# Loads of Q, K and V on a second DMA queue, ordered by a plan of both queues, in a fused attention and MLP kernel

The kernel runs on one core of one Trainium2 chip. The metric is device time of one execution in microseconds (us), median of several runs; lower is better. An execution of the kernel before takes about 333 us.

## The reference

Sliding-window attention, then an MLP whose activation is s * relu(h)^2 + b:

```python
# q, k, v: (batch 8, heads 8, seq 576, head_dim 64), float32
scores = (q @ k.T) / 8, masked to |i - j| <= 32
attn   = softmax(scores) @ v                # (8, 8, 576, 64)
x      = attn, heads side by side           # 4608 tokens x 512
h      = x @ w_in                           # 4608 x 2048
out    = (s * relu(h)**2 + b) @ w_out       # 4608 x 512
```

## The kernel before

All work is recorded as tasks (engine, cost, what it reads and writes, a key for urgency) and a planner in Python turns them into one fixed order for each engine. The order of each list is fixed when the program is built; on the chip each engine works through its list and waits on semaphores.

The dense part works in blocks of up to 512 tokens: `w<-xt,win` (TensorE, first product), `r<-w` (ScalarE, relu), `gt<-r` (VectorE, square), `o<-wout,gt` (TensorE, second product), `outs<-o` (VectorE), store. Attention is planned about two blocks ahead and stands between the dense matmuls. A batch has five units of 128 queries. From batch 2 on a batch goes this way:

```python
def load_v(b, t, key, waits=()):                 # five a batch
    add("sp", dma VST[0:n, t] <- v[b, :, 128*t : 128*t+n], 650.0, key=key, dma=("l", n // 2, 21.0), waits=waits)

def chunk(b, t0, n, key, names="qk"):            # (t0, n) = (0, 512) and (512, 64), for q and k each
    ...
    add("sp", dma stg <- src[b, :, t0:t0+n], 500.0, key=key - 20.0,
        waits=[paced(b, PACE[...])], dma=("l", np_ // 2, 53.0))
    add("dve", tensor_copy nat <- stg, 110 + 0.53 * 2048, key=key, slack=3000.0)       # f32 to bf16
    add("sp", dma transpose QT or KTR <- nat, 2200.0 if n > 64 else 1200.0, key=key + 0.1, dma=("t", np_, 22.0))
    if name == "k":
        add("pool", tensor_copy KT <- KTR, ...)  # GpSimd puts K into order, 128 columns at a time
```

`paced(b, u)` makes a load wait for an attention unit of an earlier batch, since its buffers are in use until then. After the scores come exp (ScalarE), mask (VectorE), the product with V (TensorE, `avn`), and the normalisation into one of NXN = 3 XN buffers (VectorE). From batch 3 on a DMA transpose brings XN into XT, where the dense part reads it.

The planner takes, again and again, the open task that can start first (ties by key). It guesses when a load lands with one FIFO for all hardware DMAs:

```python
def plan(self, rounds=5):
    for _ in range(rounds):
        self._order()     # start = max(engine free, ready); ready of a load's user: self.land + 100 + slack
        self._rings()     # land = start + cost + 300, then served one after the other, + 1100
```

The softmax here doesn't subtract the row's maximum and nothing guards it: scores larger than these inputs give would overflow.

## Time and profile before

| | before |
|---|---|
| median of all runs beside the changed kernel's, us | 333.0 (332.0 to 334.6) |
| span of the profiled run, us | 332.1 |
| TensorE busy, us | 305.5 |
| TensorE idle, 0 to 60 / 60 to 160 / 160 to 320 us | 13.2 / 9.4 / 0.5 |
| TensorE at half clock between 100 and 200 us | 2 x 3.4 us |
| VectorE busy / ScalarE busy / GpSimd busy, us | 204.7 / 141.1 / 59.0 |

The prediction below shows the lines of the profile that carry this. Read the idle time by stage, not as a share of the whole: the change doesn't touch the loads of batches 0 and 1 and the weights, and after 160 us TensorE hardly waits.

### The profile page before, as it was taken

To read this page: it belongs to the slowest core of one execution; us is meant where nothing else is said; L and a number is where in the kernel's file an instruction comes from. 1 tells how busy PE (TensorE), PEld (TensorE's weight loads), DVE (VectorE), ACT (ScalarE), POOL (GpSimd) and SP (SyncE) were. 2 spreads that over 40 slices of the span, in tenths; PEclk is the share of its full clock that TensorE was granted. 3 is DMA by queue.
4 is the path that set the end of the run, shared out by engine and by line. 5 is a ranking of instruction groups with operands and counts; after the bars stand their busy time and mean duration, and the time that the engine had idled before them with its cause. 6 is when DMAs were issued, how large, how long until landed. Compare 5 with 4: busy or idle time off the path is not lost.

```text
span 332.1 us, 8135 instructions
## 1 busy us (share of the span) xinstructions
PE 305.5 (92%) x3452; PEld 162.2 (49%) x3452; DVE 204.7 (62%) x396; ACT 141.1 (42%) x219; POOL 59.0 (18%) x72
## 2 busy tenths in 40 slices
PE   3687999899989996988999999999999999999995
PEld 3565787654445443433445444444544444444442
DVE  2865768857887884858667865995654443333321
ACT  4644574246435653543444444444544323333300
POOL 3446444005050004100500600040000000000000
PEclk9999999999999999899799999999999999999999
DMA  7999999899999966998899879973121111100021
GB/s 255 288 307 353 335 273 343 145 200 238 197 179 310 222 139 116 287 149 172 245 211 172 208 210 201 169 192 113 45 59 49 49 43 44 53 33 34 34 84 74
DMA packets 104581, 56.71 MB, mean 171 GB/s; under 512 B 77216, under 2 KB 96160, under 8 KB 104544
## 3 DMA queue, kind: packets, MB, share of 16 engines
q1 hardware_dynamic: 104544, 56.18, 72.8%
q8 instruction: 27, 0.44, 0.6%
q14 instruction: 10, 0.08, 0.1%
HBM read 36.70 MB, written 9.44 MB: 139 GB/s over the span
## 4 chain that ended last, share of the span: by engine, by line
PE 58%; DMA 28%; DVE 6%; issue 3%; SPq 2%; POOL 1%; ACT 1%; DVEq 0%
PE o L815 28%; PE w L797 24%; DMA stg<-in_k_dram 7%; DMA vst<-in_v_dram 6%; DMA stg<-in_moe_w_out_dram 5%; DMA xt<-xn 3%; PE avn L597 3%; DMA stg<-in_moe_w_in_dram 2%; DMA qt<-nat 2%; DVE gt L806 2%; DVE nat L504 2%; DMA ktr<-nat 1%; PE o L838 1%; PE sc L541 1%; DVE xn L619 1%
## 5 line engine op out<-in xcount | busy, mean ns | idle before, releaser
L815 PE MATMUL o<-wout,gt 128*128 128x512 bf16 (+1 forms) x640 | 146.2, 361 | 2.8 <-DVE gt L806 1.8
L797 PE MATMUL w<-xt,win 128*128 128x512 bf16 (+3 forms) x704 | 147.9, 346 | 0.9 <-ACT xt L631 0.9
L804 ACT ACTIVATE r<-w 128x512 bf16<-128x512 f32 (+2 forms) x152 | 87.2, 574 | 111.0 <-PE w L797 90.9
L806 DVE TENSOR_TENSOR gt<-r 128x512 bf16<-128x512 bf16 (+2 forms) x152 | 68.9, 459 | 69.8 <-ACT r L804 69.3
L815 PEld LDWEIGHTS o<-wout,gt 128*128 128x128 bf16 x640 | 61.6, 98 | 65.9 <-DVE gt L806 2.3
L797 PEld LDWEIGHTS w<-xt,win 128*128 128x128 bf16 x704 | 60.8, 100 | 58.5 <-issue 2.4
L518 POOL COPY kt<-ktr 128x512 bf16<-128x512 bf16 (+1 forms) x30 | 31.8, 1059 | 135.2 <-DMA ktr<-nat 134.1
L567 ACT ACTIVATE ex<-sc 128x1024 bf16<-128x1024 f32 (+1 forms) x35 | 35.7, 1021 | 35.3 <-PE avn L597 33.9
L828 DVE SCALAR_TENSOR_TENSOR outs<-o,sb,cvec 128x512 f32<-128x512 f32 (+1 forms) x40 | 27.4, 690 | 13.0 <-PE o L815 13.0
L504 DVE CAST nat<-stg 128x2048 bf16<-128x2048 f32 (+1 forms) x24 | 29.7, 1246 | 7.2 <-DMA stg<-in_k_dram 6.0
L597 PE MATMUL avn<-vb,ex 64*64 64x65 bf16 x976 | 22.1, 199 | 8.4 <-DVE xn L619 4.5
L571 DVE TENSOR_TENSOR ex<-ex,mask 128x1024 bf16<-128x1024 bf16 (+1 forms) x35 | 25.8, 739 | 2.4 <-ACT ex L567 1.1
L619 DVE TENSOR_TENSOR xn<-avn,rec 128x512 bf16<-128x512 f32 (+1 forms) x34 | 23.3, 686 | 4.7 <-DMA xt<-xn 3.9
L597 PEld LDWEIGHTS avn<-vb,ex 64*64 64x64 bf16 x976 | 14.4, 108 | 23.5 <-issue 8.7
L445 DVE CAST vb<-vst 128x512 bf16<-128x512 f32 (+1 forms) x32 | 14.5, 456 | 8.3 <-DMA vst<-in_v_dram 8.3
L541 PE MATMUL sc<-qt,kt 64*64 64x128 bf16 x504 | 14.9, 217 | 0.0
L617 DVE RECIPROCAL rec<-avn 128x8 f32<-128x8 f32 (+1 forms) x34 | 6.8, 200 | 8.1 <-PE avn L597 8.1
L465 PE MATMUL w<-ident,nat 64*64 64x64 bf16 x144 | 5.4, 239 | 6.2 <-ACT nat L458 4.5
L541 PEld LDWEIGHTS sc<-qt,kt 64*64 64x64 bf16 x504 | 9.8, 107 | 1.3 <-issue 0.9
L426 POOL CAST win<-stg 128x1024 bf16<-128x1024 f32 x8 | 8.5, 1068 | 8.9 <-DMA stg<-in_moe_w_in_dram 8.8
L631 ACT COPY xt<-avn 128x512 bf16<-128x512 bf16 (+1 forms) x9 | 4.8, 537 | 11.6 <-PE avn L626 11.6
L465 PEld LDWEIGHTS w<-ident,nat 64*64 64x64 bf16 x144 | 4.6, 151 | 6.9 <-ACT nat L458 4.5
(62 smaller groups left out, 96.8 us busy)
## 6 DMA issues: line engine op xcount, KB each, us to landing
vst<-in_v_dram SPq DMA_DIRECT2D x32, 256.0 KB, 5.4
out_dram<-outs SPq DMA_DIRECT2D x32, 256.0 KB, 2.2
stg<-in_q_dram SPq DMA_DIRECT2D x6, 1024.0 KB, 6.6
stg<-in_k_dram SPq DMA_DIRECT2D x6, 1024.0 KB, 11.2
stg<-in_moe_w_in_dram SPq DMA_DIRECT2D x8, 512.0 KB, 7.6
stg<-in_moe_w_out_dram SPq DMA_DIRECT2D x8, 512.0 KB, 9.1
stg<-in_q_dram SPq DMA_DIRECT2D x8, 288.0 KB, 5.7
stg<-in_k_dram SPq DMA_DIRECT2D x8, 288.0 KB, 6.1
```

Of the source, the lines that this page charges most:

```text
L504: add("dve", lambda e, stg=stg, nat=nat: e.tensor_copy(nat.rearrange("p (i h d) -> p h i d", h=H, i=4), stg.rearrange("p (h i d) -> p h i ...
L518: add("pool", lambda e, c=c, w=w: e.tensor_copy(KT[slot][:, :, c:c + w].rearrange("p a (s i) -> p a s i", i=4), KTR[slot][:, :, :, c // 4: ...
L541: fns = [lambda e, pr=pr, j=j, hp=hp: e.matmul(SC[64 * (j % 2):64 * (j % 2) + 64, hp, pr * 128:pr * 128 + 128], lhsT=KT[slot][64 * hp:64 * ...
L567: add("act", lambda e, dst=flat_dst, src=flat_src: e.activation(dst, src, AF.Exp, bias=0.0, scale=0.125), 190 + 0.833 * 512 * len(hs), rea ...
L571: add("dve", lambda e, flat=flat, mask=mask: e.tensor_tensor(flat, flat, mask, ALU.mult), 130 + 0.53 * 512 * len(hs), reads=[("E", ei, hp, ...
L597: return [lambda e: e.matmul(av[64 * x:64 * x + 64, h, 0:D + 1], lhsT=buf[64 * g:64 * g + 64, h % 2, h // 2, c:c + 64], rhs=VB[slot][64 * ...
L619: add("dve", lambda e: e.tensor_tensor(XN[xi][0:p1, :].rearrange("p (a c) -> p a c", a=H), av[0:p1, :, 0:D], REC[ri][0:p1, :].rearrange("p ...
L797: add("pe", [lambda e, g=g, kc=kc: e.matmul(wt[:, g, :], lhsT=WIN_BF[:, kc, (f0 + g) * 128:(f0 + g + 1) * 128], rhs=XT[:, kc, t0 % XR:t0 % ...
L804: add("act", lambda e: e.activation(rt, wt, AF.Relu, bias=0.0, scale=1.0), 190 + 0.833 * ng * nt, reads=[("W", wb)], writes=[("R1", rb)], ...
L806: add("dve", lambda e: e.tensor_tensor(GT[gs][:, f0:f0 + ng, g0:g0 + nt], rt, rt, ALU.mult), 130 + 0.53 * ng * nt, reads=[("R1", rb)], wri ...
L815: add("pe", [lambda e, fc=fc: e.matmul(O[:, ob, 0:cn], lhsT=GT[gs][:, fc, g0:g0 + 128], rhs=WOUT_BF[:, fc, c0:c0 + cn], start=(fc == 0), s ...
L828: add("dve", lambda e: e.scalar_tensor_tensor(OUTS[us][:, 0:cn], O[:, ob, 0:cn], SB128[:, 0:1], CVEC[:, c0:c0 + cn], ALU.mult, ALU.add), 2 ...
```

## The change

Its intent: the later loads shall not stand in one queue with transposes and stores, and the planner shall know what two queues do. Core of the diff (the planner's new inner functions and a few constants are cut; NTILE and the like are unchanged):

```diff
-LAG = 2
+LAG = 1                      # units between scores and their product with V
-PACE = ((-1,-1,-1,-1),(-2,-2,-2,-2),(-2,-2,-2,-2))
+PACE = ((-1, -1, -1),) * 3
+LATE = 2                     # batches from here on load from ScalarE
+CASTE = (("pool", "pool"), ("dve", "dve"))
+SLACK = (1000.0, 2000.0, 3000.0, 3000.0)
+    RING, CALM, ISSUE, WRITE = 112.0, 40.0, 1400.0, 600.0
-    def plan(self, rounds=5): ... _rings ... _order ...
+    def plan(self):
+        rings, clock, room = {"sp": [], "act": []}, [0.0], {}
+        ...  # serve(): both rings' heads share the DMA engines; a load's user becomes ready when it is served
+                    if s == "act" and t.dma is not None:
+                        at = max(at, space(s, self.CALM))     # a load only into a nearly drained ring
+        ...
+            full = max(st, space(t.stream, self.RING))        # an issue holds its engine while the ring is full
-        NSTG, NNAT, NEX, NXN, NR1, NOUT, XR = 8, 6, 5, 3, 3, 6, 2048
+        NSTG, NNAT, NEX, NXN, NR1, NOUT, XR = 8, 6, 5, 5, 3, 5, 2048
+        def late(b):
+            return "sp" if b < LATE else "act"
         def load_v(b, t, key, waits=()):
-            add("sp",
+            add(late(b),
-        def chunk(b, t0, n, key, names="qk"):
+        def piece(b, parts, key, waits):        # q 512 | k 512 | q 64 and k 64 in one staging tile
+            add(late(b), [dma of each part], ...)
+            for x in (0, 1):                    # the cast in two halves of 1024 columns
+                eng = CASTE[min(b, 3) - 2][x]
+                add(eng, tensor_copy nat half x <- stg, ...)
+            ...                                 # transposes stay on "sp"
```

More of the change, by code (lines that the diff above doesn't have):

```diff
@@ L30 @@
 XPE = 3
-PACE = ((-1,-1,-1,-1),(-2,-2,-2,-2),(-2,-2,-2,-2))
+PACE = ((-1, -1, -1),) * 3
+CASTS = 20.0
+LATE = 2
+AFTERV = 4
+KTV = 0
+CASTE = (("pool", "pool"), ("dve", "dve"))
+SLACK = (1000.0, 2000.0, 3000.0, 3000.0)
 PACEV = ((-1,-1,0,0,1),(0,0,1,1,2),(0,0,1,1,2))
@@ L97, in add @@
         return t
-    def plan(self, rounds=5):
-        self.land = {}
-        for _ in range(rounds):
-            self._order()
-            self._rings()
-    def _rings(self):
-        jobs = {"hw": [], "sw": []}
-        for t in self.order:
-            if t.dma is not None:
-                r = "sw" if t.stream == "pool" else "hw"
-                jobs[r].append([t, t.start + t.cost + (300.0 if r == "hw" else 700.0), float(t.dma[1])])
-        now, at = 0.0, {"hw": 0, "sw": 0}
-        while any(at[r] < len(jobs[r]) for r in jobs):
-            head = {r: jobs[r][at[r]] for r in jobs if at[r] < len(jobs[r])}
-            live = {r: j for r, j in head.items() if j[1] <= now}
-            if not live:
-                now = min(j[1] for j in head.values())
-                continue
-            cost = sum(j[0].dma[2] for j in live.values())
-            step = min(j[2] for j in live.values()) * cost
-            for r, j in head.items():
-                if r not in live:
-                    step = min(step, j[1] - now)
-            now += step
-            for r, j in live.items():
-                j[2] -= step / cost
-                if j[2] <= 1e-6:
-                    self.land[j[0].n] = now + 1100.0 - j[0].start
-                    at[r] += 1
-    def _order(self):
+    def plan(self):
         free = {s: 600.0 for s in self.STREAMS}
@@ L140, in _order @@
         order = []
-        while len(order) < len(self.tasks):
-            best = None
-            for s in self.STREAMS:
-                for t in open_[s]:
-                    c = (max(free[s], t.ready), t.key, t.n)
-                    if best is None or c < best[0]:
-                        best = (c, t)
-            assert best is not None, "a cycle"
-            (st, _, _), t = best
-            open_[t.stream].remove(t)
-            t.start = st
-            free[t.stream] = st + t.cost
-            t.fin = st + t.cost
-            if t.dma is not None:
-                t.fin = st + self.land.get(t.n, t.cost + 1800.0 + t.dma[1] * t.dma[2])
-            order.append(t)
-            for u in t.next:
-                u.left -= 1
-                if u.left == 0:
-                    open_[u.stream].append(u)
+        rings, clock, room = {"sp": [], "act": []}, [0.0], {}
@@ new lines, in serve @@
+        def serve(rings, now, until, jobs=None):
+            while now < until - 1e-6:
+                live = {r: q[0] for r, q in rings.items() if q and q[0][1] <= now + 1e-6}
+                later = [q[0][1] for q in rings.values() if q and q[0][1] > now + 1e-6]
+                if not live:
+                    if not later:
+                        return None, until
+                    now = min(later + [until])
+                    continue
+                cost = sum(j[0].dma[2] for j in live.values())
+                step = min([j[2] * cost for j in live.values()] + [x - now for x in later] + [until - now])
+                now += step
+                for r, j in live.items():
+                    j[2] -= step / cost
+                    if j[2] < 1e-4:
+                        rings[r].pop(0)
+                        return j[0], now
+            return None, until
@@ new lines, in space @@
+        def space(s, most):
+            if (s, most) not in room:
+                copy, now = {r: [list(j) for j in q] for r, q in rings.items()}, clock[0]
+                while sum(j[2] for j in copy[s]) > most + 1e-3:
+                    head = copy[s][0]
+                    over = sum(j[2] for j in copy[s]) - most
+                    if over >= head[2]:
+                        _, now = serve(copy, now, 1e9)
+                    else:
+                        want = head[2] - over
+                        while copy[s] and copy[s][0] is head and head[2] > want + 1e-6:
+                            _, now = serve(copy, now, now + 50.0)
+                room[s, most] = now
+            return room[s, most]
@@ L161, in _order, with release @@
+        def release(t):
             for u in t.users:
@@ L173, in _order @@
                     open_[u.stream].append(u)
+        while len(order) < len(self.tasks):
+            best = None
+            for s in self.STREAMS:
+                for t in open_[s]:
+                    at = max(free[s], t.ready)
+                    if s == "act" and t.dma is not None:
+                        at = max(at, space(s, self.CALM))
+                    c = (at, t.key, t.n)
+                    if best is None or c < best[0]:
+                        best = (c, t)
+            st = best[0][0] if best else 1e9
+            done, clock[0] = serve(rings, clock[0], max(st, clock[0]))
+            room.clear()
+            if done is not None:
+                done.fin = clock[0] + self.WRITE
+                release(done)
+                continue
+            assert best is not None, "a cycle"
+            t = best[1]
+            open_[t.stream].remove(t)
+            t.start = st
+            free[t.stream] = t.fin = st + t.cost
+            order.append(t)
+            for u in t.next:
+                u.left -= 1
+                if u.left == 0:
+                    open_[u.stream].append(u)
+            if t.dma is None:
+                release(t)
+                continue
+            full = max(st, space(t.stream, self.RING))
+            if t.dma[0] == "t":
+                free[t.stream] = full + t.cost
+            else:
+                free[t.stream] = max(st + t.cost, full)
+            rings[t.stream].append([t, (full if t.dma[0] == "t" else st) + self.ISSUE, float(t.dma[1])])
+            room.clear()
         self.order = order
+        while any(rings.values()):
+            done, clock[0] = serve(rings, clock[0], 1e9)
+            done.fin = clock[0] + self.WRITE
     def emit(self, sems):
@@ L432, in paced @@
             return land["av", b - 1, u] if u >= 0 else land["av", b - 2, NUNIT + u]
+        def late(b):
+            return "sp" if b < LATE else "act"
         def load_v(b, t, key, waits=()):
             n = min(128, S - 128 * t)
-            add("sp",
+            add(late(b),
                 lambda e: e.dma_start(VST[0:n, t, :, :], v[b, :, 128 * t:128 * t + n, :].rearrange("h p d -> p h d")),
-                650.0, writes=[("VST", t)], key=key, dma=("l", n // 2, 21.0), waits=waits)
+                650.0, writes=[("VST", t)], key=key, dma=("l", n // 2, 23.0), waits=waits)
             land["v", b, t] = g.tasks[-1]
@@ L481, in q_later @@
             return QTS[b % 2].rearrange("p (i a) s -> p i a s", i=4)
-        def chunk(b, t0, n, key, names="qk"):
-            slot, np_, s0 = b % 2, n // 4, t0 // 4
-            if b < 4 and t0 == 0 and "q" in names:
+        def piece(b, parts, key, waits):
+            slot = b % 2
+            ring["stg"] += ring["stg"] % 2
+            ring["nat"] += ring["nat"] % 2
+            si, _ = take("stg", NSTG), take("stg", NSTG)
+            ni, _ = take("nat", NNAT), take("nat", NNAT)
+            stg = STGS[:, si:si + 2, :].rearrange("p x c -> p (x c)")
+            nat = NATS[:, ni:ni + 2, :].rearrange("p x c -> p (x c)")
+            stgr, natr = [("STG", si), ("STG", si + 1)], [("NAT", ni), ("NAT", ni + 1)]
+            top = max(p0 + n // 4 for _, _, n, p0 in parts)
+            add(late(b), [lambda e, name=name, t0=t0, n=n, p0=p0: e.dma_start(
+                stg[p0:p0 + n // 4, :].rearrange("p (h c) -> p h c", h=H),
+                src_of[name][b, :, t0:t0 + n, :].rearrange("h (p i) d -> p h (i d)", i=4))
+                for name, t0, n, p0 in parts],
+                500.0 * len(parts), writes=stgr, key=key - 20.0, waits=waits,
+                dma=("l", sum(n for _, _, n, _ in parts) // 8, 68.0))
+            for x in (0, 1):
+                eng = CASTE[min(b, 3) - 2][x]
+                add(eng, lambda e, x=x: e.tensor_copy(
+                    nat[0:top, 1024 * x:1024 * x + 1024].rearrange("p (i h d) -> p h i d", h=H, i=2),
+                    stg[0:top, :].rearrange("p (h i d) -> p h i d", h=H, i=4)[:, :, 2 * x:2 * x + 2, :]),
+                    110 + (0.53 if eng == "dve" else 1.05) * 1024, reads=stgr, writes=[("NAT", ni + x)], key=key + CASTS, slack=SLACK[0])
+            for name, t0, n, p0 in parts:
+                np_, s0, xs = n // 4, t0 // 4, pieces(t0, t0 + n, 64)
+                dst = q_later(b)[:, :, :, 16 + s0:16 + s0 + np_] if name == "q" else KTR[slot][:, :, :, s0:s0 + np_]
+                add("sp", lambda e, dst=dst, p0=p0, np_=np_: e.dma_start(
+                    dst.rearrange("p i a s -> p (i a) s"), nat[p0:p0 + np_, :], transpose=True),
+                    2000.0 if n > 64 else 1200.0, reads=natr,
+                    writes=[("QT", slot, x, pr) for x in xs for pr in range(NPAIR)] if name == "q" else [("KTR", slot, t0)],
+                    key=key + 0.1, dma=("t", np_, 20.0))
+                if name == "q":
+                    continue
+                land["kt", b, t0] = g.tasks[-1]
+                for c in range(t0, t0 + n, 128):
+                    w = min(128, t0 + n - c)
+                    add("pool", lambda e, c=c, w=w: e.tensor_copy(
+                        KT[slot][:, :, c:c + w].rearrange("p a (s i) -> p a s i", i=4),
+                        KTR[slot][:, :, :, c // 4:(c + w) // 4].rearrange("p i a s -> p a s i")),
+                        100 + 5.5 * w, reads=[("KTR", slot, t0)],
+                        writes=[("KT", slot, x, pr) for x in pieces(c, c + w, 64) for pr in range(NPAIR)],
+                        key=key + 3.0, slack=SLACK[1])
@@ L487, in chunk, with later @@
+        def later(b, key):
+            slot = b % 2
+            if b < 4:
                 for c0, x in ((0, 0), (160, WIN + S)):
@@ L490, in chunk @@
                         key=key - 20.0)
-            for name in names:
-                ring["stg"] += ring["stg"] % 2
-                ring["nat"] += ring["nat"] % 2
-                si, _ = take("stg", NSTG), take("stg", NSTG)
-                ni, _ = take("nat", NNAT), take("nat", NNAT)
-                stg = STGS[0:np_, si:si + 2, :].rearrange("p x c -> p (x c)")
-                nat = NATS[0:np_, ni:ni + 2, :].rearrange("p x c -> p (x c)")
-                stgr, natr = [("STG", si), ("STG", si + 1)], [("NAT", ni), ("NAT", ni + 1)]
-                add("sp", lambda e, stg=stg, name=name: e.dma_start(
-                    stg.rearrange("p (h c) -> p h c", h=H),
-                    src_of[name][b, :, t0:t0 + n, :].rearrange("h (p i) d -> p h (i d)", i=4)),
-                    500.0, writes=stgr, key=key - 20.0,
-                    waits=[paced(b, PACE[min(b, 4) - 2][2 * (t0 > 0) + "qk".index(name)])], dma=("l", np_ // 2, 53.0))
-                add("dve", lambda e, stg=stg, nat=nat: e.tensor_copy(
-                    nat.rearrange("p (i h d) -> p h i d", h=H, i=4), stg.rearrange("p (h i d) -> p h i d", h=H, i=4)),
-                    110 + 0.53 * 2048, reads=stgr, writes=natr, key=key, slack=3000.0)
-                dst = q_later(b)[:, :, :, 16 + s0:16 + s0 + np_] if name == "q" else KTR[slot][:, :, :, s0:s0 + np_]
-                xs = pieces(t0, t0 + n, 64)
-                add("sp", lambda e, nat=nat, dst=dst: e.dma_start(
-                    dst.rearrange("p i a s -> p (i a) s"), nat, transpose=True),
-                    2200.0 if n > 64 else 1200.0, reads=natr,
-                    writes=[("QT", slot, x, pr) for x in xs for pr in range(NPAIR)] if name == "q" else [("KTR", slot, t0)],
-                    key=key + 0.1, dma=("t", np_, 22.0))
-                if name == "k":
-                    land["kt", b, t0] = g.tasks[-1]
-                    for c in range(t0, t0 + n, 128):
-                        w = min(128, t0 + n - c)
-                        add("pool", lambda e, c=c, w=w: e.tensor_copy(
-                            KT[slot][:, :, c:c + w].rearrange("p a (s i) -> p a s i", i=4),
-                            KTR[slot][:, :, :, c // 4:(c + w) // 4].rearrange("p i a s -> p a s i")),
-                            100 + 4.8 * w, reads=[("KTR", slot, t0)],
-                            writes=[("KT", slot, x, pr) for x in pieces(c, c + w, 64) for pr in range(NPAIR)],
-                            key=key + 3.0, slack=2000.0)
@@ L527, in bass_sliding_window_symmetric__then__act_starrelu_kernel @@
+            for i, parts in enumerate(((("q", 0, 512, 0),), (("k", 0, 512, 0),), (("q", 512, 64, 0), ("k", 512, 64, 32)))):
+                piece(b, parts, key + 0.01 * i, [paced(b, PACE[min(b, 4) - 2][i])] +
+                      ([land["v", b - 1, AFTERV]] if b > (1 if LATE == 2 else 2) and AFTERV >= 0 else []))
         ucount = {"n": 0}
@@ L638, in finish @@
                         XT[:, :, a0 % XR:a0 % XR + a1 - a0], XN[xi][p0 + a0 - x0:p0 + a1 - x0, :], transpose=True),
-                        200.0 + 1050.0 * (a1 - a0) / 128, reads=[("XN", xi)], writes=xt_res(a0, a1), key=key,
+                        1230.0, reads=[("XN", xi)], writes=xt_res(a0, a1), key=key,
                         dma=("t", (a1 - a0) // 4, 22.0))
@@ L650, in pe_part @@
                     reads=[r for p in parts for r in p[1]], writes=[r for p in parts for r in p[2]], key=key,
-                    slack=1500.0, waits=waits)
+                    slack=1500.0 if key < due(2, 0) - 1 else SLACK[2], waits=waits)
             t.mark = mark
@@ L760, in attention @@
             for b in range(2, B):
-                for t0, n in ((0, 512), (512, 64)):
-                    chunk(b, t0, n, due(b, 0) - 24.0)
+                later(b, due(b, 0) - 24.0)
                 for t in range(NUNIT):
-                    load_v(b, t, due(b, t) - 35.0, waits=[paced(b, PACEV[min(b, 4) - 2][t])] + ([land["kt", 2, 0]] if b == 2 else []))
-                    cast_v(b, t, due(b, t) - 4.0, EV2[t], 3000.0)
+                    load_v(b, t, due(b, t) - 35.0, waits=[paced(b, PACEV[min(b, 4) - 2][t])] + ([land["kt", 2, 0]] if b == 2 and KTV else []))
+                    cast_v(b, t, due(b, t) - 4.0, EV2[t], SLACK[3])
                 for u in range(NUNIT):
```

## The prediction

> **What bounds the kernel now.** I read the page first, for the shares and the 40 slices, then TensorE's busy time in ten-microsecond windows, then the waits between 56 and 166 us, then the timeline around the largest of them.
>
> ```profile
> PE 305.5 (92%) x3452; PEld 162.2 (49%) x3452; DVE 204.7 (62%) x396; ACT 141.1 (42%) x219; POOL 59.0 (18%) x72
> ...
> PE   3687999899989996988999999999999999999995
> ...
> PEclk9999999999999999899799999999999999999999
> DMA  7999999899999966998899879973121111100021
> ```
>
> TensorE is the bound: 305.5 of 332.1 us. So the most that anything can win without touching the matmuls is its idle time of 26.6 us, plus time at a lowered clock. The slices (8.3 us each) show where it sits: in the first 40 us, at the very end, and in slices 10 to 19. In the ten-microsecond windows the idle time adds up to 13.2 us in 0 to 60, 9.4 us in 60 to 160, 0.5 us in 160 to 320, and 3.5 us after that (the last matmul's tail and the last store). The DMA row is full up to about 230 us and nearly empty after it: loads run ahead of their use late, and behind it in the middle.
>
> ```profile
> 120.00:130.00 10.00, 7.21 (x78) 3.21 (x76) 4.30 (x10) 3.94 (x6) 4.38 (x4) 1.00 0.67 114
> 130.00:140.00 10.00, 9.07 (x153) 4.38 (x153) 8.23 (x17) 4.37 (x6) 0.87 (x1) 0.83 0.98 275
> 140.00:150.00 10.00, 8.39 (x83) 3.80 (x76) 6.10 (x13) 5.34 (x8) 0.00 (x0) 1.00 1.15 147
> 150.00:160.00 10.00, 8.22 (x82) 3.79 (x81) 7.03 (x16) 3.39 (x6) 2.60 (x3) 0.96 0.81 171
> ...
> 131.88:135.29 3.41, 3.41 (x10) 1.20 (x9) 2.95 (x6) 0.82 (x2) 0.87 (x1) 0.50 0.83 222
> 159.19:162.60 3.41, 3.41 (x20) 1.06 (x20) 2.93 (x5) 1.57 (x2) 2.72 (x3) 0.50 0.88 231
> ```
>
> The columns are the stretch, its length, busy time of PE, weight load, DVE, ACT and POOL, the clock, and DMA's share and rate. TensorE idles 2.79, 0.93, 1.61 and 1.78 us here, and twice a stretch of 3.41 us at clock 0.50 follows: 1.7 us lost in each, although the engine counts as busy. Middle-stage loss: 9.4 + 3.4 = 12.8 us. That is my ceiling for this stage.
>
> What ends those idle times, in 56 to 166 us (total, times, longest):
>
> ```profile
> DVE vb L445 <- DMA vst<-in_v_dram: 7.6, 5, 3.6
> ...
> PE avn L597 <- DVE xn L619: 4.1, 3, 2.3
> ...
> DVE xn L619 <- DMA xt<-xn: 3.9, 1, 3.9
> ...
> PE avn L597 <- POOL kt L518: 3.0, 2, 1.8
> ...
> PE o L815 <- DVE gt L806: 1.6, 2, 1.3
> ```
>
> Three causes, all behind one DMA queue. V comes late, VectorE stands still on its cast, and the normalisation behind it holds TensorE. A transpose into XT has not yet given back one of three XN buffers. K's transposes come late, so that GpSimd's reordering copy is late. The first as it happened:
>
> ```profile
> 128.69 1.25 SPq L438 DMA_DIRECT2D vst<-in_v_dram  x2
> 129.62 0.43 DVE L445 CAST vb<-vst 128x512 bf16<-128x512 f32 x1 [3.65 <-DMA vst<-in_v_dram]
> 129.96 0.68 DVE L619 TENSOR_TENSOR xn<-avn,rec 128x512 bf16<-128x512 f32 x1
> ...
> 130.70 0.25 PE L597 MATMUL avn<-vb,ex 64*64 64x65 bf16 x6 [2.30 <-DVE xn L619]
> ```
>
> VectorE waits 3.65 us for V, TensorE 2.30 us for VectorE, and 1.2 us later the clock is halved.
>
> SyncE's own timeline says why the loads are late: from 60 to 170 us its issues add up to 102 of 110 us. The same transpose of 128 rows, qt<-nat or ktr<-nat, takes between 1.93 and 6.67 us to issue, so most of that is waiting for room in the queue, and everything behind it waits too. Loads are 31.3 us of the 102 (V 18.9, Q 7.3, K 5.1), transposes 62.9, stores 8.1.
>
> **What the Trainium skill says.** "DMA: Bandwidth & Descriptors", section "Issuing engines are not separate DMA queues", holds that all issuers share the same 16 engines and that a second issuer only saves sequencer time, "usually small relative to the DMA itself". The first half fits: DMA's share is already 0.99 over 60 to 170 us, so I expect no more bandwidth. The second doesn't: here sequencer time is 102 of 110 us. The same page, "Queues, rings and completion order", gives SyncE and ScalarE a ring each, served in turn; no run before uses two, so that is untested here. It also warns ("Silent corruption: two transposing streams in flight at once") against transposes from two issuers; the change leaves all on SyncE, so no risk. "TensorE: Matmul & The Clock Gate", section "What's actually happening", gives a window of 3413 ns and half clock after idleness; the two stretches of 3.41 us at 0.50 agree, though the idle time before them was shorter than a whole window.
>
> **The change, part by part.**
>
> Loads of Q, K, V for batches 2 to 7 move to ScalarE: 6 x (Q, K, two tails, five V) = 54 issues. SyncE keeps transposes and stores, losing 31.3 of its 102 us in that stage. V and K no longer stand behind transposes. Worth the wait through V (2.3 us of the 4.1) and most of the K wait (3.0 us).
>
> The planner orders everything with a model of both rings in place of one. The built program's order shows the effect, and this is my main evidence. Counting only the dense matmuls in front (0.216 us for 512 columns: the chain has four in 0.86 us), batch 4's first scores stand behind 105.8 us of such work where they stood behind 97.7; batch 5's 139.1 (123.2), batch 6's 171.5 (153.0), batch 7's 203.0 (187.9). Attention is 8 to 18 us later among dense work, exactly where TensorE waited for it. For batch 4, Q was issued at 101.1 us before and its scores ran at 125.0, 1.2 us late: 24 us were a little too few. After, ScalarE issues it at the start of batch 3's attention, 28 us of dense work ahead plus the attention's own; batch 5 gets 33, where 27 (131.3 to 158.4) were too few.
>
> Five XN buffers (NOUT pays, 6 to 5): the 3.9 us of VectorE behind an XT transpose goes, and with it 1.6 us of TensorE (the third piece of the 4.1).
>
> Casts. Before, 24 on VectorE: 12 x 1.296 + 12 x 1.197 = 29.9 us; a tail of 16 partitions costs as much as 128. After, Q's and K's tails share one cast, and each is cut in halves of 1024 columns: 5 batches x 3 x 2 = 30 on VectorE, estimated at 0.65 us each (half of 1.296) = 19.5 us. Batch 2's six go to GpSimd at 1.07 us (its cast of 128x1024) = 6.4 us, on an engine that is 18% busy. VectorE gains 10 us, off the path, but a GT square no longer stands behind a whole 1.2 us cast: half of the 1.6 us wait, 0.8.
>
> Clock: fewer idle stretches, so most of the 3.4 us; I take 2.5.
>
> Lag 1 in place of 2, and batch 1's attention placed differently among the second-half products: I allow 1.0 us, the wait for the issue in batch 1 at 58.7 us (1.03 in the chain).
>
> Cost: 54 issues on ScalarE at 0.57 us (an unhindered load on SyncE at that stage) = 31 us on an engine with 141 busy of 332; in 60 to 170 us it goes from 51 of 110 us to about 72. Mostly beside other work: its evacuation r<-w waited 90.9 us in 100 cases for TensorE, 0.9 us a case, more than one issue. But exp (1.02) + issue (0.57) + evacuation (0.60) is 2.2 us where two W banks cover 1.7. I charge 2.0 us.
>
> Sum: 2.3 + 3.0 + 1.6 + 0.8 + 2.5 + 1.0 - 2.0 = 9.2 us. 332.9 - 9.2 = 323.7.
>
> **Rivals.** First: DMA capacity is the true limit. For: share 0.99 and no byte less to move; transposes may crawl beside loads. Against: from 160 us on TensorE hardly waits at that same share, and DMA ends at about 230 us, 100 us early. Then only buffers, casts and order pay: about 329. Second: ScalarE becomes the new in-order trap. A load that waits for its buffer or for ring room there (SyncE's V issues took up to 3.05 us) holds evacuations, and TensorE stops after two banks. For: 54 chances. Against: the plan issues a load only when the ring is nearly drained. It would give back 4 to 8 us: 328 to 332, or slower with clock losses on top. Third: everything works and ScalarE costs nothing: the ceiling of 12.8 and something before 60 us, about 319.
>
> **Range and chances.** Main path 323.7, pulled towards the third by the size of the shift in the order, towards the second by the untested ring: range 318 to 329.5. The 2% line is 326.25. Faster 0.70, within 2% 0.27, slower 0.03.
>
> **What would show it.** Right: PE's slices 10 to 19 read 9 throughout, the clock row has at most one dip, no wait of VectorE on xt<-xn, waits on kt and vst near zero on TensorE's path, a second hardware queue, SyncE's issues well under 100 us in 60 to 170. DVE's casts fall to about 20 us. PE busy stays within 305 plus or minus 3 us. Wrong: r<-w evacuations released by ScalarE's own DMA issues with TensorE idle behind them, loads landing far later than 11 us, or TensorE idle for over 15 us in the first 60 (13.2 before), because the early V and Q loads of batch 2 take rate from the weights.

## The result

The changed kernel takes 323.3 us (median of 4, 322.3 to 324.1) against 333.0 (4 runs). The ratio is 0.970, 95% interval 0.966 to 0.975. Here and below a ratio is the mean time of one kernel's fast runs over that of the other's of the same rounds, so not quite the ratio of the medians. (A run more than 1.5% above the fastest of its kernel counts as slow and is left out.)

The page after, the same rows as in the prediction, and the DMA queues:

```profile
PE 295.8 (92%) x3410; PEld 160.8 (50%) x3452; DVE 206.6 (64%) x402; ACT 141.2 (44%) x219; POOL 66.1 (21%) x78
...
PE   2776999999998999999999999999999999999995
...
PEclk9999999999999999999999999999999999999999
DMA  7999999897995999789929994999312210000021
...
q1 hardware_dynamic: 62208, 34.94, 46.0%
q10 hardware_dynamic: 42336, 21.24, 28.8%
```

The dips of slices 10 to 19 are gone but for one 8 near 100 us, and so is the lowered clock; a second queue carries 21 of 56 MB. One trap: PE busy has fallen by 9.7 us although no matmul was removed. At most 3.4 us of it is the half clock that is gone. For the rest: 3410 matmul records stand beside 3452 weight loads, so 42 records, all of dense matmuls, are missing from this trace. A busy sum that fell without a cause is to be checked so before it is believed.

The same four stretches, with the columns as before:

```profile
120.00:130.00 10.00, 9.52 (x44) 4.24 (x44) 5.23 (x14) 3.58 (x6) 0.00 (x0) 1.00 1.33 189
130.00:140.00 10.00, 9.00 (x116) 4.54 (x116) 9.07 (x15) 5.32 (x8) 5.55 (x5) 1.00 0.75 232
140.00:150.00 10.00, 9.68 (x172) 4.97 (x171) 7.97 (x18) 5.59 (x9) 0.00 (x0) 1.00 1.03 165
150.00:160.00 10.00, 9.84 (x63) 4.59 (x58) 6.18 (x13) 2.15 (x3) 0.55 (x1) 1.00 1.14 225
```

TensorE now idles 0.5, 1.0, 0.3 and 0.2 us here by the records, some of it missing records. In the list of waits between 56 and 166 us there is no wait of VectorE on V or on an XT transpose any more, and what TensorE itself waits for begins with

```profile
PE w L849 <- issue: 1.5, 8, 0.4
...
PE avn L650 <- ACT xt L684: 1.0, 1, 1.0
```

To see when the time was won, I gave each matmul in each kernel's order its undisturbed cost (an estimate from the chain of before: 0.216 us per 512 columns of dense work, 0.027 us a score matmul, 0.011 us a product with V) and asked when TensorE got to the same sum of work. The weight loads, whose records are complete, give the times:

| TensorE work done, us | before at, us | after at, us | gained |
|---|---|---|---|
| 40 | 59.7 | 60.4 | -0.7 |
| 70 | 91.2 | 91.0 | 0.2 |
| 100 | 125.0 | 122.8 | 2.2 |
| 110 | 139.3 | 133.6 | 5.7 |
| 130 | 164.6 | 154.4 | 10.2 |
| 290 | 326.5 | 315.8 | 10.8 |

Practically all of it is won between 115 and 165 us, where batches 4 and 5 enter. Nothing is won before 90 us.

Is the data there earlier? The page gives the time from issue to landing:

```profile
vst<-in_v_dram SPq DMA_DIRECT2D x32, 256.0 KB, 5.4
...
stg<-in_q_dram SPq DMA_DIRECT2D x6, 1024.0 KB, 6.6
stg<-in_k_dram SPq DMA_DIRECT2D x6, 1024.0 KB, 11.2
```

before, and after, with the issuing queue ACTq:

```profile
vst<-in_v_dram ACTq DMA_DIRECT2D x24, 256.0 KB, 5.5
stg<-in_q_dram ACTq DMA_DIRECT2D x6, 1024.0 KB, 5.5
stg<-in_k_dram ACTq DMA_DIRECT2D x6, 1024.0 KB, 8.0
```

K's load alone lands 3 us sooner. But K is of use only when GpSimd reorders it, after load, cast and transpose. From K's issue to the first of those copies it took 22.3, 25.3, 23.4 and 21.0 us before for batches 4 to 7 (K's issue in SyncE's timeline, the copy in GpSimd's; mean 23.0), and 24.7, 25.0, 25.4 and 23.0 us after (mean 24.5). **The path from load to use has not become shorter with two rings.** (A ring is here one issuing engine's DMA queue.) The path is not bare transfer time: batch 4's K landed at 113.2 us in the changed kernel, its cast came up at 116.2, its transpose at 122.3, and that landed at 130.4.

What K's load gained, its transpose lost. From start of issue to landing, the four large transposes of K of batches 4 to 7 took 4.4 to 5.6 us before and 7.6 to 10.0 us after; in e1 below, with the order of the changed kernel on one ring, they took 4.4 to 5.5 us, and K's load landed in a median of 8.5 us there too. This is what the first rival of the prediction named: transposes may crawl beside loads. The unchanged path was the first sign that my story of the queue was not the right one.

### The profile page after: what moved, and what is told of

It reads as the page before. It is cut to its first block, busy times and chain, and to the rows that moved or that the text cites. A ratio compares the mean times of both kernels' runs of the same rounds, so it can differ in the third digit from the quotient of the medians.

```text
span 321.4 us, 8084 instructions
## 1 busy us (share of the span) xinstructions
PE 295.8 (92%) x3410; PEld 160.8 (50%) x3452; DVE 206.6 (64%) x402; ACT 141.2 (44%) x219; POOL 66.1 (21%) x78
## 4 chain that ended last, share of the span: by engine, by line
PE 78%; DMA 9%; DVE 5%; issue 3%; ACT 2%; ACTq 1%; SPq 1%; POOL 0%
PE o L867 35%; PE w L849 34%; PE avn L650 4%; DMA stg<-in_moe_w_out_dram 3%; DMA vst<-in_v_dram 3%; DMA stg<-in_moe_w_in_dram 2%; PE sc L594 2%; DVE gt L858 1%; DVE ex L624 1%; PE o L890 1%; DVE xn L672 1%; DVE outs L880 1%; DMA stg<-in_q_dram 1%; PE sc L505 1%; ACT r L856 1%
## 5 line engine op out<-in xcount | busy, mean ns | idle before, releaser
L849 PE MATMUL w<-xt,win 128*128 128x512 bf16 (+3 forms) x679 | 139.6, 341 | 5.5 <-issue 2.8
L867 PE MATMUL o<-wout,gt 128*128 128x512 bf16 (+1 forms) x623 | 139.6, 357 | 5.1 <-DVE wout L462 2.5
L858 DVE TENSOR_TENSOR gt<-r 128x512 bf16<-128x512 bf16 (+2 forms) x152 | 75.5, 503 | 67.3 <-ACT r L856 66.7
L620 ACT ACTIVATE ex<-sc 128x1024 bf16<-128x1024 f32 (+1 forms) x35 | 35.8, 1023 | 30.7 <-PE avn L650 24.1
L624 DVE TENSOR_TENSOR ex<-ex,mask 128x1024 bf16<-128x1024 bf16 (+1 forms) x35 | 26.6, 760 | 5.5 <-ACT ex L620 4.6
L672 DVE TENSOR_TENSOR xn<-avn,rec 128x512 bf16<-128x512 f32 (+1 forms) x34 | 23.4, 688 | 0.8
L485 DVE CAST vb<-vst 128x512 bf16<-128x512 f32 (+1 forms) x32 | 20.1, 632 | 0.0
L543 DVE CAST nat<-stg 128x1024 bf16<-128x1024 f32 (+1 forms) x30 | 19.7, 677 | 0.0
L462 POOL CAST wout<-stg 128x1024 bf16<-128x1024 f32 x6 | 6.6, 1096 | 8.6 <-DMA stg<-in_moe_w_out_dram 8.6
```

The lines of the kernel that those rows point to most:

```text
L485: (lambda e: e.tensor_copy(VB[slot][0:n, t, :, 0:D], VST[0:n, t, :, :])),
L620: add("act", lambda e, dst=flat_dst, src=flat_src: e.activation(dst, src, AF.Exp, bias=0.0, scale=0.125), 190 + 0.833 * 512 * len(hs), rea ...
L624: add("dve", lambda e, flat=flat, mask=mask: e.tensor_tensor(flat, flat, mask, ALU.mult), 130 + 0.53 * 512 * len(hs), reads=[("E", ei, hp, ...
L672: add("dve", lambda e: e.tensor_tensor(XN[xi][0:p1, :].rearrange("p (a c) -> p a c", a=H), av[0:p1, :, 0:D], REC[ri][0:p1, :].rearrange("p ...
L849: add("pe", [lambda e, g=g, kc=kc: e.matmul(wt[:, g, :], lhsT=WIN_BF[:, kc, (f0 + g) * 128:(f0 + g + 1) * 128], rhs=XT[:, kc, t0 % XR:t0 % ...
L858: add("dve", lambda e: e.tensor_tensor(GT[gs][:, f0:f0 + ng, g0:g0 + nt], rt, rt, ALU.mult), 130 + 0.53 * ng * nt, reads=[("R1", rb)], wri ...
```

## The experiments

Theory A is my prediction's: the second ring frees loads, so K and V come in time. Theory B: the order that the plan gives is what counts, the ring little. The table has all twelve runs (6 each, 5 rounds); short diffs and readings follow.

| run | median us | ratio to before | 95% interval |
|---|---|---|---|
| changed kernel | 323.3 | 0.970 | 0.966 to 0.975 |
| e1 changed kernel's order, one ring | 324.1 | 0.971 | 0.964 to 0.979 |
| e2 order of before, two rings | 338.9 | 1.012 | 1.005 to 1.019 |
| e3 changed kernel, three XN | 323.4 | 0.968 | 0.962 to 0.974 |
| e4 before, five XN | 334.6 | 1.000 | 0.992 to 1.007 |
| e5 order of before, two rings from batch 4 | 331.4 | 0.995 | 0.987 to 1.003 |
| e6 before, paced later | 333.6 | 0.998 | 0.991 to 1.006 |
| e7 changed kernel, planned for one ring | 325.9 | 0.977 | 0.969 to 0.984 |
| e8 changed kernel, lag 2 | 328.8 | 0.984 | 0.977 to 0.991 |
| e9 all new but the planner, one ring | 332.4 | 0.992 | 0.987 to 0.997 |
| e10 changed kernel, old casts | 324.4 | 0.967 | 0.962 to 0.973 |
| e11 changed kernel, loads 8 us later | 363.0 | 1.082 | 1.076 to 1.088 |
| e12 before, lag 1 | 336.3 | 1.005 | 1.001 to 1.009 |

The kernel before had medians of 334.1 to 336.2, so ratios are to be compared, not medians. All twelve were correct.

**e1: the ring taken away, the order kept.** After planning, the loads are handed back to SyncE; the built orders of TensorE, VectorE and GpSimd are identical line by line, and ScalarE's lacks only the 54 issues.

```diff
         g.plan()
+        for t in g.order:
+            if t.stream == "act" and t.dma is not None:
+                t.stream = "sp"
```

> The changed kernel with its plan kept, so that PE, DVE, GpSimd and ScalarE's compute have the very same order, but the 54 later loads are issued from SyncE at the same place of the plan. Theory A (the second ring is what frees the loads, because they no longer stand behind transposes): most of the 10 us comes back, 329 to 333 us, with waits on V and K and half clock in 100 to 170 us. Theory B (the later place of attention in TensorE's order is enough): 322 to 325 us, no half clock.

0.971, the same as with two rings within an interval of about 0.75% either way. K's issue to the first reorder copy took 23.7, 21.5, 23.1 and 20.2 us for batches 4 to 7 (mean 22.1). VectorE now waits for V, which the changed kernel never does, but TensorE has dense work in front:

```profile
DVE vb L485 <- DMA vst<-in_v_dram: 4.2, 3, 3.1
```

Theory A falls: one ring carries this order as well as two, as far as these intervals can tell. SyncE's issues add up to 83.7 us in 60 to 170 us here, against 67.5 in the changed kernel.

**e2: the ring added, the order kept.** The reverse, in the kernel before:

```diff
         g.plan()
+        for t in g.order:
+            if t.stream == "sp" and t.dma is not None and t.dma[0] == "l" and t.key > -100:
+                t.stream = "act"
```

> The kernel before with its own plan kept, but the 54 later loads are issued from ScalarE at the same place of the plan. Theory A: 323 to 327 us, since the loads land earlier and K and V no longer keep TensorE waiting. Theory B: 330 us or more, since attention still stands too early among the dense matmuls; ScalarE may also be held at loads whose buffers aren't free, then 334 or more.

Slower, by my second rival in the prediction: a load on ScalarE holds what stands behind it. ScalarE's timeline:

```profile
50.34 0.41 ACT L804 ACTIVATE r<-w 128x288 bf16<-128x288 f32 x1
58.94 0.35 ACTq L499 DMA_DIRECT2D stg<-in_q_dram  x1
59.34 1.02 ACT L567 ACTIVATE ex<-sc 128x1024 bf16<-128x1024 f32 x1 [8.59 <-POOL wout L426]
```

The issue itself takes 0.35 us, but it waits for a staging buffer that GpSimd empties only then, and the exp behind it stands 8.59 us. TensorE starves and its clock is halved (first 50 to 57 us, then 57 to 64 us; the eighth value is the clock):

```profile
50.00:57.00 7.00, 3.98 (x72) 3.27 (x70) 2.29 (x5) 0.74 (x2) 1.74 (x3) 1.00 1.11 335
57.00:64.00 7.00, 3.59 (x61) 2.74 (x62) 2.54 (x5) 2.42 (x3) 4.00 (x4) 0.51 0.43 142
```

By the table of work, it is 11.3 us behind the kernel before at 60 us of work and 5.5 at the end: it makes up 5.8 later on. That could be the ring, or the lead that the loads gained from the stall. Hence e5.

**e3 and e4: the XN buffers.** `NXN` 5 to 3 in the changed kernel (same order on every engine), and 3 to 5 (NOUT 6 to 5) in the kernel before.

> The changed kernel with three XN buffers in place of five; the order is the same on every engine. If the buffers carry what I charged to them: 1.6 us or more slower, 325 us, with VectorE waiting on the XT transposes. If the new order alone took that wait away: within 0.5 us of the changed kernel.

> The kernel before with five XN and five output buffers (the plan moves a few instructions with it). If XN is a cause by itself: 1.6 us faster and no wait of VectorE on xt<-xn, perhaps 3 us faster if one of the two half-clock stretches goes too. If it is only one of several waits in one queue: within 1 us, because K or V comes late in its place.

0.968 and 1.000: nothing either way. In e4 the wait of VectorE on the XT transpose (3.9 us before) is gone and both stretches of half clock are still there; TensorE waits 4.6 us for K's copies there in place of 3.0. In e3 the wait doesn't return at all. So the wait goes with the order, and in the new order three buffers are enough.

**e5: the ring from batch 4 on, old order.** As e2, for the 36 loads of batches 4 to 7 only.

> The run with the old order and two rings was spoilt by ScalarE standing still at batch 2's and 3's loads (7 us of half clock near 57 us), and that delay itself gave the loads a lead. Here the old plan is kept again and only the 36 loads of batches 4 to 7 are issued from ScalarE, so that everything up to about 95 us is as in the kernel before. If the second ring helps by itself: 325 to 328 us, with K and V no longer waited for from 100 to 160 us. If the place of attention in TensorE's order is what counts: within 2 us of before (331 to 335), with the waits of 120 to 160 us still there.

0.995 with 1 inside the interval. The 331.4 us lie in the range that I gave for theory B (331 to 335), but the interval is too wide to decide. K's issue to the first copy took 22.3 us for batch 4 and 26.6 for batch 5 (22.3 and 25.3 before), so the second ring does not shorten that path here either. A small gain of the ring with the old order can't be excluded.

**e6: attention later, by pacing alone.**

```diff
-PACE = ((-1,-1,-1,-1),(-2,-2,-2,-2),(-2,-2,-2,-2))
+PACE = ((-1,-1,-1,-1),)*3
```

> The kernel before with one constant changed: Q and K loads of batch 3 and later wait for the last unit two batches earlier, not the last but one, as in the changed kernel. One ring, three XN buffers, whole casts, lag 2. Its plan then puts batch 5's first scores behind 110.8 us of dense work in place of 100.4, batch 6's behind 139.3 (126.3), batch 4's behind 83.1 (78.8). If the later place of attention is the cause: 325 to 329 us, no half clock after batch 5's start, though loads are issued later. If order matters only together with the ring: 331 us or more, since the loads come later still.

0.998: no gain, although batch 5 now stands 10 us of dense work later. The profiled run (332.4 us) has no half clock after the first 23 us either, so the clock's return alone doesn't bring the gain. This kills the simple form of theory B, "later is better". Loads and attention both moved, and the gap between did not suit. The copy of K and the first product behind it, batch 4:

```profile
131.13 4.45 POOL L518 COPY kt<-ktr 128x512 bf16<-128x512 bf16 x4 [29.59 <-DMA ktr<-nat]
...
132.23 0.32 PE L597 MATMUL avn<-vb,ex 64*64 64x65 bf16 x16 [1.77 <-POOL kt L518]
```

The scores start within 0.6 us of the end of the first copy (1.07 us) in each of batches 4 to 7, and TensorE waits for K three times there (4.1 us in all). In the changed kernel batch 4's K takes the same 24.7 us from issue to copy as in e6, but there is dense work up to just then:

```profile
130.46 2.30 POOL L560 COPY kt<-ktr 128x512 bf16<-128x512 bf16 x2 [28.07 <-DMA ktr<-nat]
...
131.91 0.17 PEld L650 LDWEIGHTS avn<-vb,ex 64*64 64x64 bf16 x9 [0.42 <-POOL kt L560]
131.91 0.25 PE L650 MATMUL avn<-vb,ex 64*64 64x65 bf16 x6
```

The engine is not idle before that matmul; only the weight load waited 0.42 us. So the theory becomes B2: what counts is how much work the order puts between a load's issue and its first use, measured against the 20 to 28 us that the data takes in these runs.

**e11: the test of B2.** The changed kernel's plan, each load moved back on ScalarE by up to 8 us of planned time, never past its first user; all other engines have the same order.

```diff
         g.plan()
+        order = list(g.order)
+        for t in (the 54 loads, last first):
+            move t in order behind every task that starts within 8000 of it, up to its first user or the next load
+        g.order = order
```

> The changed kernel with its plan kept, every later load issued from ScalarE up to 8 us later in the plan (2 to 8 instructions of ScalarE later, never behind its first user). PE, DVE, GpSimd and SyncE have the very same order. If what counts is the lead from load to use, the waits on K and V come back: 327 to 332 us, with half clock. If what counts is the place of attention in TensorE's order alone: within 1 us of the changed kernel.

363 us: by the ratios (1.082 over 0.970) 11.5% over the changed kernel, with the same matmuls in the same order. Its waits from 56 to 240 us:

```profile
DVE vb L485 <- DMA vst<-in_v_dram: 22.4, 11, 4.1
DVE nat L543 <- DMA stg<-in_k_dram: 16.5, 5, 6.8
DVE nat L543 <- DMA stg<-in_q_dram: 16.2, 4, 4.5
...
PE o L867 <- DVE gt L858: 9.9, 5, 4.2
PE avn L650 <- DVE ex L624: 9.2, 4, 4.2
```

VectorE stands in its own list on casts whose data isn't there, and behind them stand squares and masks that TensorE needs. Half clock adds up to 23.9 us between 60 and 300 us. I had expected 327 to 332; my reading, not tested, is that each late batch delays the units on which the next loads are paced, so that the loss is paid again. Direction as B2 has it, size far above.

**e7 and e9: the planner by itself, on one ring.** e7 is the changed kernel with `LATE = 8`, so that no batch loads from ScalarE, planned anew. e9 is e7 with the old planner put back.

> The changed kernel with all loads on SyncE's ring, planned anew for that one ring by the new planner (batch 4's first scores behind 85.7 us of dense work, batch 5's behind 110.8, batch 6's 137.5). If a plan that knows the ring's speed is the cause: 323 to 327 us. If the second ring carries more than the earlier run with the same order showed: 329 us or more.

> The changed kernel's casts, lag 1, pacing and five XN buffers on one ring, ordered by the planner of before. It differs from the run planned anew for one ring (0.9765 of before) in the planner alone. Its order puts batch 4's first scores behind 82.3 us of dense work (85.7 there), batch 5's 109.9 (110.8), batch 6's 133.2 (137.5). If the ring model in the planner is the cause: 330 us or more. If casts, lag and pacing are: 324 to 327 us, as with the new planner.

0.977 against 0.992, with intervals that don't overlap: casts, lag, pacing and buffers are the same in both. The planner alone is worth about 1.5% of the time before, 5 us. e9 still has the old picture between 56 and 240 us:

```profile
PE avn L621 <- POOL kt L531: 5.3, 2, 3.1
```

and 10.2 us of half clock after 100 us, where e7 has none. Batch 4's K needs 24.5 us from issue to copy in e9 and 24.1 in e7: the same path, another amount of work in front. SyncE is as busy in e7 as in the kernel before (102.9 us of issues in 60 to 170 us, against 102.3), and most of the gain is there. e7 is 0.6% behind the changed kernel; their intervals overlap, so whether planning for two rings is worth that I can't say.

**The same by batch.** The planner's own guess can be had by running it in each kept kernel. The table has K's time from issue to first reorder copy, as planned and as measured in the profiled run, in us:

| kernel (ratio) | batch 4 | batch 5 | batch 6 | batch 7 |
|---|---|---|---|---|
| before | 21.5, took 22.3 | 22.7, took 25.3 | 25.3, took 23.4 | 24.9, took 21.0 |
| e6 (0.998) | 22.3, took 24.7 | 25.3, took 26.3 | 25.9, took 27.9 | 25.3, took 26.5 |
| e9 (0.992) | 21.2, took 24.5 | 24.5, took 25.9 | 24.1, took 25.0 | 25.5, took 23.7 |
| e7 (0.977) | 24.4, took 24.1 | 22.8, took 19.6 | 25.2, took 24.2 | 24.1, took 21.9 |
| changed (0.970) | 24.7, took 24.7 | 26.3, took 25.0 | 26.2, took 25.5 | 26.1, took 23.0 |

The old planner's guess is too short for batches 4 and 5 (by 0.8 to 3.3 us), and in e6 and e9 for 6 as well; the new one's is not, in these two kernels. (It is no strict rule: in e10 the new planner is 1.7 us short at batch 5, without a loss in the median.) Accordingly, TensorE had 21.3, 22.2 and 22.1 us of work (estimated with the costs above) between the issue of batch 4's K and its first scores in the kernel before, e6 and e9, and 25.5 and 25.0 in e7 and the changed kernel. The stretch of 10 us of work in which batch 4 enters took 16.3 us in e9 and 10.2 in e7. That is the whole difference of the two profiled runs: for batches 5 to 7 e7 has less work in front than e9 (19.2 to 22.1 us against 23.7 to 30.6), and from there on they lose about the same. So between these two runs B2 is seen at batch 4 alone. What was not run is the old planner with only its guess made longer.

**e10: the casts.** Tails apart, whole casts of 2048 columns, all on VectorE, in the changed kernel.

> The changed kernel with the casts of before: Q's and K's tails each alone, whole casts of 2048 columns, all on VectorE, planned anew (order within 4 us of the changed kernel's). My prediction charged 0.8 us to the casts, so 324 us; if the 10 us of VectorE that they free are on the path somewhere, 327 us or more.

0.967: nothing. The 10 us of VectorE that the change frees are not on the path.

**e8 and e12: the lag.** `LAG` 1 to 2 in the changed kernel, 2 to 1 in the kernel before.

> The changed kernel with lag 2. Batch 5's scores come behind 118.5 us of dense work in place of 115.9, batch 6's 149.6 (144.4), batch 7's 181.6 (172.1). If lag 1 is part of the gain: 325 us or more. If only the later place of scores and loads counts: within 1 us of the changed kernel.

> The kernel before with lag 1 in place of 2 and nothing else (planned anew by the old planner, batch 4's first scores stay behind 78.8 us of dense work, batch 6's move from 126.3 to 133.2). If lag 1 gains by itself what lag 2 cost the changed kernel (1.4%): 328 to 330 us. If the lead from load to use is the cause and lag matters only for the plan it is in: 331 us or more, with the waits for loads between 100 and 160 us still there.

In the changed kernel lag 2 costs 1.4 percentage points (0.984), and in the kernel before lag 1 gains nothing (1.005, slightly slower). The loss in e8 begins near 103 us, where TensorE waits 2.6 us for a normalisation on VectorE and the clock is half for 6.8 us; I have not followed why that order brings it. Lag is a part of the gain only inside the new plan.

No version beats the changed kernel clearly: e3 and e10, at 0.968 and 0.967, lie within its interval. They say that three XN buffers and the simpler casts would do as well.

## Why the prediction was right, and which of its steps were not

The time (323.7 predicted, 323.3 measured) came out right, and so did the likelier outcome (faster, 0.70). The ceiling was right, too: 12.8 us to win in the middle stage, 10 won there. The terms of the sum fared worse than their total.

- **V and K waits, 5.3 us "worth" to the loads' move to ScalarE.** The waits went, as said. The cause was not the move: e1 has the loads back on SyncE, the same order, and the same time. SyncE's issues fell from 102 to 67.5 us in 60 to 170 us, and this bought nothing that shows: in e7 they are 102.9 us again, at 0.977. The step that failed: I took a queue that is always issuing for the thing that made the data late. On either number of rings K takes 20 to 25 us from issue to use, and the old plan had allowed 0.8 and 2.7 us too little of it for batches 4 and 5. That the long issues of transposes are waits for room in the queue is not shown either: 16 of Q and K took 40.8 us to issue before and 42.9 us with the loads gone from SyncE.
- **"My main evidence", the order.** This carries the result (e7 against e9: 5 us for the planner alone). Two corrections. The sums of work in front that I gave as dense alone (and the 28 and 33 us between two batches) included attention's own matmuls at a rough cost; counted by dense work alone, batches 4 to 7 move by 7.8, 15.5, 18.1 and 14.7 us, so the shifts stand. And lateness is not what helps (e6); the distance from load to use is (e11, and the table by batch).
- **XN, 1.6 us.** None (e3, e4). The wait went with the new order, whatever the number of buffers.
- **Casts, 0.8 us.** None that shows (e10). The half cast, estimated at 0.65 us, took 0.68 on the mean.
- **Clock, 2.5 us.** All 3.4 came back: no half clock from 22 to 321 us in the profiled run. (In e6 it came back without a gain.)
- **Lag, 1.0 us, placed at 58 us.** Wrong in place: nothing is won before 90 us. In size the lag is worth 1.4 points in the new plan and nothing alone.
- **ScalarE, minus 2.0 us.** Over-charged. An issue took 0.48 us on the mean (16.3 us for 34 in 60 to 170 us), not 0.57, and with the same order one ring is no faster than two, so no cost shows. This holds for this plan; e2 shows the trap that I named as the second rival, at 8.6 us for one load.

Of the signs that I named, two failed: one slice reads 8, and PE busy left its range (295.8 us), for lack of records and by the clock.

So the total was right in part by luck, and in part because one change, the order, ended all these waits: I split them into V, K, XN and lag and priced each by the wait it showed.

Open: which element of the new planner makes its guess long enough (the shared service of the rings, the held issue when a ring is full, the rule on a nearly drained ring), what lag 1 contributes to it, and whether a second ring gains a little with the old order (e5).

## What to carry to other kernels

In a fixed order on in-order engines, measure the time from a load's issue to its first use by the compute engine, and compare it with the work that the order puts in between; a planner that guesses this time too short makes every downstream engine look guilty in turn. Before crediting a second queue, run the new order on the old queue and the old order on the new one: both are a few lines once the order is a list. And a load on an engine that also computes must only stand where its buffer is sure to be free.

## What the Trainium skill lacked or had wrong

- "DMA: Bandwidth & Descriptors", section "Issuing engines are not separate DMA queues": right where my prediction said it wasn't. It holds that a second issuer saves only sequencer time; SyncE's issues in 110 us fell from 102 to 67.5 us with two rings and to 83.7 us with the same order on one, and the time was the same (0.970 and 0.971). What this section lacks is the price of a load that has to wait for its buffer on an engine that also computes: in e2 one load on ScalarE held an exp for 8.59 us.
- No page has the number that decided here: load, cast, transpose and reorder of K (1 MB) took 20 to 25 us from issue to first use with the DMA share near 1.0, on one ring or two (means 22.1 to 24.5 us in e1, the kernel before and the changed one), where landing alone took 7 to 11 us; nor has one what a second ring did to K's transposes (7.6 to 10.0 us from issue to landing, against 4.4 to 5.6 on one).
- "TensorE: Matmul & The Clock Gate", section "What's actually happening", gives half clock after at least one idle window of about 3.4 us. In the kernel before the clock was halved at 131.88 us, after no idle stretch longer than the 2.30 us that the prediction shows; at 159.19 us after a longest wait of 1.8 us. In the 3.41 us before each, TensorE was busy for 0.95 and 1.63 us, so a window need not be wholly idle. Stretches of half clock were 3.41 us or a multiple (6.83; 10.24 near the start of e10), as the page's window has it.
- "SBUF — State Buffer", section "Who interferes with whom", says that GpSimd and a VectorE operation in a mode with two ports, which a cast can be in, block each other for a whole instruction. The traces agree: a V cast of 64x512 that takes 0.42 us in e6 took 1.30 us in the changed kernel while GpSimd copied K; there, 11 V casts beside such a copy took 1.05 us on the mean and 19 beside nothing on GpSimd 0.42 us. This moved VectorE's V casts from 14.5 to 20.1 us in all, without a loss that shows.

```profile
131.61 2.39 POOL L560 COPY kt<-ktr 128x512 bf16<-128x512 bf16 x2
131.75 1.30 DVE L485 CAST vb<-vst 64x512 bf16<-64x512 f32 x1
```
